# Six chunks of the first batch requested at once, mixing weights ahead of the stores, 17 unread products, and a second batch whose first stage is taken in another order

## The chip, the cores and the metric

The kernel runs on one core of a Trainium2 chip. A core has TensorE (matrix products, PE), VectorE (DVE), ScalarE (ACT), GpSimd (POOL) and SyncE (SP), which here issues nearly all transfers; 16 DMA engines carry them out. Each engine works through its own instructions in order, and semaphores tell one engine of another's progress. The metric is the device time of one execution in microseconds; less is better.

## The reference

`x` has 8 batches of 2496 rows by 256 columns. Each batch goes through a Fourier transform along its rows, a complex mix of the columns with a bias, a soft threshold and the inverse transform. The rows that come out go each to the best of eight experts.

```python
X = np.fft.rfft(x, axis=1)
Yr = Xr @ w_r - Xi @ w_i + b_r
Yi = Xr @ w_i + Xi @ w_r + b_i
Yr = np.sign(Yr) * np.maximum(np.abs(Yr) - 0.01, 0.0)   # Yi likewise
y = np.fft.irfft(Yr + 1j * Yi, n=2496, axis=1)
...
logits = x @ w_gate + modality_bias[modality_id]        # x: all rows of y
e_idx = np.argmax(logits, axis=1)
out[mask] = gate_w[mask, None] * (np.maximum(x[mask] @ w1[e], 0.0) @ w2[e])   # for each expert e
```

All values are float32.

## The kernel before, in words

The first part of the program does the transforms, the mix and the routing for batch after batch; the second part runs 78 tiles of expert products. The change lies in the start of the first part, which handles batches 0 and 1.

The 2496 points are split as 39 x 64. **Stage 1** (`s1_chunk`, products on L254) transforms over the 39. It uses that rows n and 39 - n go in as a sum and a difference: the host lays the rows out in pairs (`fold_rows`), `fold_load` brings a chunk of them (L221), and `fold` makes sum (VectorE, L233) and difference (L234, on VectorE for odd chunks and on GpSimd for even ones). A batch has six chunks: chunk 0 has one row pair a partition, the others two. The sum of a chunk is written into a part of the tile of the chunk before it that is no longer needed. Chunk tiles come from the pool `wx` with five buffers, so a sixth request waits until one is free. ScalarE copies the products of a chunk to `ev` (L256), and after each odd chunk SyncE stores them to the scratch tensor `scr` in DRAM (L262): four stores after chunk 1, four after chunk 3, six after chunk 5.

**Stage 2** works on ten pairs of frequencies a batch. `a_load` brings the rows of a pair back from `scr` (L275), with four buffers; the rows of any pair need all stores of the batch. `s2_pair` multiplies them by a part of the table `c_m` (L284); ScalarE and VectorE take the result apart into `Us`, `Xh` and `Xl` (L291 to L294). `mix_shared` (L307) and `mix_own` (L315) are the complex mix with the weights `wmix_r` and `wmix`, `shrink` is the threshold (L322, L323), and `is2_group` (L338, product `zs`) starts the inverse with a part of the table `c_q`. What follows in each batch (L352 to L409) ends the inverse and prepares the routing.

The mixing weights are made by `consts_mix`, a generator: its first part asks for `w_r`, `w_i` and the two biases, each bias being one row that is read once for each of 128 partitions; its second part is seven VectorE instructions (L203 to L208).

What sets the order: on TensorE, ScalarE, VectorE and GpSimd the order is that of the code in `build` (a manual schedule). On SyncE a scheduler places the transfers, bound by the data and by `issue_after`, which puts a request behind a named one. Five chunks of batch 0 are asked for first; chunk 5 and the first part of `c_m` behind the first four stores; chunks 0 to 3 of batch 1 between and behind further stores; then weights, biases and the first rows of stage 2. The code that follows takes chunks 0 to 2 of batch 1 between the first pairs, and the loop `for g in range(5)` takes chunks 3, 4 and 5 in its passes 0, 1 and 2, one a pass, behind `s2` of pairs 4, 6 and 8.

Of the kernel before, what the change touches and what calls it, by code (L numbers as in the profile page):

```python
# [23 lines left out]
D = 256  # L24
# [104 lines left out]
def fold_rows(x):  # L129
# [3 lines left out]
    out = np.zeros((nb, 128, 2, J1, d), x.dtype)  # L133
    for h in range(2):
        for g in range(3):
            p, o = HF * h + 21 * g, (3 * h + g) * J1
            n = min(J1, N2 - o)
            out[:, p:p + K1, 0, :n] = x[:, :K1, o:o + n]
            out[:, p + 1:p + 1 + K1, 1, :n] = x[:, :N1 - 1 - K1:-1, o:o + n]
    return out  # L140


class Attn:
# [5 lines left out]
    def pools(self, ctx):  # L149
# [5 lines left out]
        self.wx = pool("wx", 5)  # L155
# [38 lines left out]
    def consts_mix(self):  # L194
# [5 lines left out]
        for i, nm in enumerate(("b_r", "b_i")):  # L200
            nc.sync.dma_start(self.bias[:, i, :], I[nm].rearrange("(o d) -> o d", o=1).to_broadcast([128, 256]))
        yield
# [14 lines left out]
    def fold_load(self, b, c):  # L217

        lo, hi = max(0, 2 * c - 1), 2 * c + 1
        self.xt[b, c] = self.wx.tile([128, 2, 2, D], F32, tag="x", name=f"x_{b}_{c}"), hi - lo  # L220
        return self.nc.sync.dma_start(self.xt[b, c][0][:, :, :hi - lo, :], self.I["x"][b, :, :, lo:hi, :])  # L221

    def fold(self, b, c):
# [5 lines left out]
        a, z = (x[:, i, :n].rearrange("p j d -> p (j d)") for i in range(2))  # L229
# [968 lines left out]
def build(tc, I, out, nb):  # L1198
    nc = tc.nc
    with ExitStack() as outer:  # L1200
        dp = outer.enter_context(tc.tile_pool(name="wsp", bufs=1, space=DRAM))
        wsp = dp.tile([E * 128, 8192], F32, name="wsp")
        with ExitStack() as ctx:
# [7 lines left out]
            def spare(name):  # L1211
                pool = next(rooms)
                if pool is at.wx:
                    return pool.tile([128, 2, 2, D], F32, tag="x", name=name).rearrange("p i j d -> p i (j d)")
# [33 lines left out]
            for c in range(5):  # L1248
                first = at.fold_load(0, c)
            at.fold(0, 0)  # L1250
            at.fold(0, 1)
            mixing = at.consts_mix()
            for c in range(6):
                at.s1_chunk(0, c)
                at.fold(0, c + 2)
                with tc.issue_after(at.stored.ins if c else first.ins):
                    if c == 1:
                        at.fold_load(0, 5)
                        at.table_load("m", 0)
                    elif c == 3:  # L1260
                        at.fold_load(1, 0)
                        at.fold_load(1, 1)
                    elif c == 5:
                        at.fold_load(1, 2)
                        ins = at.fold_load(1, 3)
            with tc.issue_after(at.stored.ins):
                next(mixing, None)
                for i in range(3):
# [245 lines left out]
```

## Time and profile before

| | us |
|---|---|
| median of 3 runs | 1478.58 |
| lowest and highest | 1478.58, 1480.11 |
| profiled execution | 1481.04 |
| its span, first to last instruction | 1479.3 |
| TensorE busy in it | 1399.1 (95%) |
| VectorE, ScalarE, GpSimd busy | 774.5, 580.1, 552.6 |

The span is cut into stretches by the starts of named steps. What counts in a stretch is how long TensorE waited in it, for whom, and which of its two clock levels was granted: a clock of 1.00 means 2.4 GHz, of 0.50 means 1.2 GHz, and a value between them is a mean over the stretch. A DMA share of 1 means that all 16 engines had packets under way all the time. Times in the profile count from the first instruction.

### The profile page before, as it was taken

Reading aid. Unit: us, or ns where it says so; the run is one execution under the profiler, and the core shown is the slowest. Engines: PE = TensorE matmul, PEld = TensorE weight load, DVE = VectorE, ACT = ScalarE, POOL = GpSimd, SP = SyncE. Lnnn points to the kernel's source line nnn. Section 1 sums busy time; section 2 is a strip of 40 time slices with the busy share of each in tenths; the row PEclk is TensorE's granted clock in tenths of the full one; section 3 lists DMA queues with packets and bytes.
Section 4 is the critical chain, followed back from the end, with each engine's and each line's share of the span. In section 5 each row is a group of like instructions: output and inputs, shape, how many; then the busy total and the mean of one; then the engine's idle time right before and its main releaser. Section 6 shows DMA issues by size and latency. Waiting matters only on the chain. (4 is left out here: it accounts for less than half of the span.)

```text
span 1479.3 us, 34745 instructions
## 1 busy us (share of the span) xinstructions
PE 1399.1 (95%) x13058; PEld 1264.6 (85%) x13058; DVE 774.5 (52%) x1427; ACT 580.1 (39%) x1127; POOL 552.6 (37%) x562
## 2 busy tenths in 40 slices
PE   3899999999999896999999999999999999999998
PEld 1777685859586783999998999999999999999998
DVE  2567766656666774555664554554343433434332
ACT  2445454554545462333343333333232333323332
POOL 1012555556465554555232332232222323223222
PEclk7899999999999997999999999999999999999999
DMA  8745464545545475765565688883522222264520
GB/s 254 229 128 179 137 193 135 180 148 162 168 147 155 153 274 158 260 190 162 165 197 144 172 255 252 269 252 67 161 45 44 59 44 48 54 207 119 159 45 31
DMA packets 305163, 229.34 MB, mean 155 GB/s; under 512 B 203998, under 2 KB 259040, under 8 KB 302432
## 3 DMA queue, kind: packets, MB, share of 16 engines
q1 hardware_dynamic: 285120, 185.46, 44.4%
q0 software_dynamic: 19872, 41.61, 7.9%
q8 instruction: 105, 1.72, 0.5%
q14 instruction: 66, 0.54, 0.1%
HBM read 417.59 MB, written 112.54 MB: 358 GB/s over the span
## 5 line engine op out<-in xcount | busy, mean ns | idle before, releaser
L948 PE MATMUL y<-w,hh 128*128 128x256 f32 x2496 | 431.8, 277 | 1.9 <-DMA w<-wsp 1.6
L918 PE MATMUL h<-xh,w 128*128 128x256 f32 x2496 | 402.4, 278 | 6.5 <-DMA w<-wsp 3.6
L948 PEld LDWEIGHTS y<-w,hh 128*128 128x128 f32 x2496 | 376.7, 188 | 4.3 <-issue 2.1
L918 PEld LDWEIGHTS h<-xh,w 128*128 128x128 f32 x2496 | 339.1, 189 | 8.7 <-issue 4.2
L948 PE MATMUL y<-w,hl 128*128 128x256 f32 x1248 | 345.9, 277 | 0.4 <-issue 0.2
L573 POOL DMA_INDIRECT xs<-x,si x256 | 257.0, 1004 | 224.3 <-PE bk L398 45.4
L921 DVE SCALAR_TENSOR_TENSOR hl<-h,hh 128x512 fp32r<-128x512 f32 x312 | 214.6, 690 | 170.2 <-ACT hh L920 121.8
L920 ACT ACTIVATE hh<-h 128x512 fp32r<-128x512 f32 x312 | 185.9, 599 | 259.9 <-PE h L918 247.7
L963 POOL DMA_INDIRECT out<-o,ix x157 | 154.6, 984 | 326.7 <-ACT o L940 286.0
L918 PE MATMUL h<-xl,w 128*128 128x256 f32 x1248 | 245.2, 278 | 0.0
L948 PEld LDWEIGHTS y<-w,hl 128*128 128x128 f32 x1248 | 234.3, 188 | 0.9 <-DVE hl L921 0.4
L938 DVE TENSOR_SCALAR o<-y,xt 128x256 f32<-128x256 f32 x78 | 37.8, 484 | 299.3 <-ACT o L940 295.2
L918 PEld LDWEIGHTS h<-xl,w 128*128 128x128 f32 x1248 | 189.4, 189 | 0.2 <-DVE xl L899 0.2
L899 POOL TENSOR_TENSOR xl<-tr,xh 128x512 fp32r<-128x512 f32 x72 | 93.2, 1295 | 242.0 <-ACT xh L898 242.0
L940 ACT ACTIVATE o<-y,xt 128x256 f32<-128x256 f32 x78 | 37.1, 476 | 282.0 <-PE y L948 279.2
L315 PE MATMUL mx<-wmix,Xh 128*128 128x256 f32 x640 | 106.4, 289 | 1.9 <-issue 1.2
L284 PE MATMUL s<-c_m,a 128*128 128x128 f32 x640 | 87.6, 281 | 17.1 <-DMA a<-scr 14.1
L284 PEld LDWEIGHTS s<-c_m,a 128*128 128x128 f32 x640 | 82.0, 194 | 22.9 <-issue 18.1
L315 PEld LDWEIGHTS mx<-wmix,Xh 128*128 128x128 f32 x640 | 87.5, 192 | 14.7 <-issue 8.9
L338 PE MATMUL zs<-c_q,s 64*128 64x128 f32 x1280 | 85.2, 282 | 6.2 <-ACT z L342 4.8
L889 DVE STREAM_TRANSPOSE tr<-xt 128x512 f32<-128x512 f32 x78 | 90.1, 1155 | 0.0
L338 PEld LDWEIGHTS zs<-c_q,s 64*128 64x128 f32 x1280 | 76.6, 191 | 12.6 <-ACT z L342 4.9
(213 smaller groups left out, 1482.2 us busy)
## 6 DMA issues: line engine op xcount, KB each, us to landing
w<-wsp SPq DMA_DIRECT2D x152, 2048.0 KB
wsp<-wr SPq DMA_DIRECT2D x64, 512.0 KB
x<-in_x SPq DMA_DIRECT2D x40, 512.0 KB
a<-scr SPq DMA_DIRECT2D x80, 256.0 KB
xt<-xs SPq DMA_DIRECT2D x312, 64.0 KB
wr<-in_moe_w SPq DMA_DIRECT2D x64, 256.0 KB
scr<-ev SPq DMA_DIRECT2D x48, 240.0 KB
pw<-in_moe_w SPq DMA_DIRECT2D x8, 1024.0 KB
```

The costliest lines, as they stand in the source:

```text
L284: self.done = nc.tensor.matmul(ps[:, c, :, i, :], at[:, i, c * 128:(c + 1) * 128], self.m[:, k1 * 128:(k1 + 1) * 128].rearrange("p (r k) - ...
L315: self.done = self.nc.tensor.matmul(ps[:, i, :], t[:, c, 1 - i, :], self.w[:, i, c, lo, :], start=False, stop=n == len(ops) - 1, skip_grou ...
L338: self.done = nc.tensor.matmul(ps[i][:, h, c, :], s[rows, r, c * 128:(c + 1) * 128], self.q[rows, o:o + 128], start=r == 0, stop=r == 1)
L573: i = self.nc.gpsimd.indirect_dma_start(out=self.xs, out_offset=bass.IndirectOffsetOnAxis(ap=si[:, k:k + 1], axis=0), in_=rows, in_offset= ...
L889: nc.vector.transpose(tr.rearrange("p c (t s) -> p c s t", t=32), t.rearrange("p (s c e) -> p c s e", c=2, e=32))
L899: (nc.gpsimd if i > 5 else nc.vector).tensor_sub(xl, tr, xh)
L918: self.done = nc.tensor.matmul(ps[:, q, :], w1[:, lo, c, f * 128:(f + 1) * 128], x[:, c, :], start=n == 0, stop=n == 5)
L920: nc.scalar.activation(hh[:, 2 * p:2 * p + 2, :], ps, AF.Relu)
L921: nc.vector.scalar_tensor_tensor(hl[:, 2 * p:2 * p + 2, :], ps, 0.0, hh[:, 2 * p:2 * p + 2, :], ALU.max, ALU.subtract)
L938: nc.vector.tensor_scalar_mul(o[:, s, :], y[s], gate)
L948: nc.tensor.matmul(y[s], lhsT, w2[:, lo, f, :], start=n == 0, stop=n == 23)
L963: ins = self.nc.gpsimd.indirect_dma_start(out=self.out, out_offset=bass.IndirectOffsetOnAxis(ap=ix, axis=0), in_=o, in_offset=None, bounds ...
```

## The change

`fold_rows` lays out x so that a chunk is one run of 4 KB a partition (2 KB for chunk 0) instead of two runs, and the host does that ahead of the kernel. `wx` has six buffers. All six chunks of batch 0 are asked for at the start; behind them come the first part of `c_m`, the weights and the biases, and only then the stores. Behind chunk 5 TensorE does 17 products of `c_m` with itself (`warm`) into a PSUM tile that nobody reads. Of batch 1 nothing is asked for until the rows of pair 2 are; its chunks 0 and 1 come behind `s2` of pair 3, chunks 2 to 5 in the passes 0 and 1 of the loop, two a pass.

```diff
-        self.wx = pool("wx", 5)
+        self.wx = pool("wx", 6)
...
-        self.xt[b, c] = self.wx.tile([128, 2, 2, D], F32, tag="x", name=f"x_{b}_{c}"), hi - lo
-        return self.nc.sync.dma_start(self.xt[b, c][0][:, :, :hi - lo, :], self.I["x"][b, :, :, lo:hi, :])
+        self.xt[b, c] = self.wx.tile([128, 4 * D], F32, tag="x", name=f"x_{b}_{c}"), hi - lo
+        return self.nc.sync.dma_start(self.xt[b, c][0][:, :2 * (hi - lo) * D], self.I["x"][b, :, 2 * lo * D:2 * hi * D])
...
-        t, self.room = self.room[:, :n * D], x[:, 0].rearrange("p j d -> p (j d)")
+        t, self.room = self.room[:, :n * D], x[:, 2 * D:] if n == 1 else x[:, :2 * D]
...
+    def warm(self, n):
+
+        ps = self.ps.tile([128, 512], F32, tag="z", name="warm")
+        for _ in range(n):
+            self.nc.tensor.matmul(ps[:, :256], self.m[:, :128], self.m[:, :256], start=True, stop=True)
...
-            for c in range(5):
-                first = at.fold_load(0, c)
+            for c in range(6):
+                ins = at.fold_load(0, c)
+
+            def then(f, *args):
+                nonlocal ins
+                with tc.issue_after(ins.ins):
+                    ins = f(*args)
+
+            mixing = at.consts_mix()
+            then(at.table_load, "m", 0)
+            then(next, mixing)
             at.fold(0, 0)
             at.fold(0, 1)
-            mixing = at.consts_mix()
             for c in range(6):
                 at.s1_chunk(0, c)
                 at.fold(0, c + 2)
-                with tc.issue_after(at.stored.ins if c else first.ins):
...
+            ins = at.stored
+            at.warm(17)
+            next(mixing, None)
+            for f, *args in ((load, 0), (load, 1), (at.table_load, "q", 0), (load, 2), (at.table_load, "m", 1),
+                             (at.fold_load, 1, 0), (at.fold_load, 1, 1), (load, 3), (at.table_load, "m", 2),
+                             (at.fold_load, 1, 2), (at.fold_load, 1, 3), (at.fold_load, 1, 4), (at.fold_load, 1, 5)):
+                then(f, *args)
...
+            s2(0)
+            bias(0)
+            s2(1)
+            bias(1)
+            shared(0)
             s2(2)
+            shared(1)
             mix(0)
             bias(2)
+            at.fold(1, 0)
             mix(1)
             bias(3)
             s2(3)
+            at.fold(1, 1)
+            at.s1_chunk(1, 0)
+            at.fold(1, 2)
+            at.s1_chunk(1, 1)
+            at.fold(1, 3)
...
-                    if b == 0 and g < 3:
-                        at.s1_chunk(1, g + 3)
-                        at.fold(1, g + 5)
+                    if b == 0 and g < 2:
+                        at.s1_chunk(1, 2 * g + 2)
+                        at.fold(1, 2 * g + 4)
...
+                    if b == 0 and g < 2:
+                        at.s1_chunk(1, 2 * g + 3)
+                        at.fold(1, 2 * g + 5)
```

In the names below the first number behind `x`, `a`, `s1`, `s2` or `ev` is the batch, the second the chunk or pair, the last only numbers the tile. SyncE's requests from the last stores of batch 0 on, before:

```order
L262 DMA scr_0_147<-ev_0_4_1_208 60x2x256 x2
L262 DMA scr_0_147<-ev_0_4_0_207 60x4x256 x2
L262 DMA scr_0_147<-ev_0_4_1_208 40x2x256 x2
L221 DMA x_1_2_231<-in_x 128x2x512
L221 DMA x_1_3_233<-in_x 128x2x512
L198 DMA wmix_r_127<-in_w_r 128x2x256
L199 DMA st_w0_235<-in_w_i 128x2x256
L201 DMA bias_129<-in_b_r 128x256
L201 DMA bias_129<-in_b_i 128x256
L275 DMA a_0_0_241<-scr_0_147 128x2x256
```

And now, from the weights on:

```order
L200 DMA wmix_r_127<-in_w_r 128x2x256
L201 DMA st_w0_145<-in_w_i 128x2x256
L203 DMA bias_129<-in_b_r 128x256
L203 DMA bias_129<-in_b_i 128x256
L264 DMA scr_0_156<-ev_0_0_0_157 60x3x256 x2
L264 DMA scr_0_156<-ev_0_0_1_158 60x3x256 x2
L264 DMA scr_0_156<-ev_0_2_0_183 60x4x256 x2
L264 DMA scr_0_156<-ev_0_2_1_184 60x4x256 x2
L264 DMA scr_0_156<-ev_0_4_1_210 60x2x256 x2
L264 DMA scr_0_156<-ev_0_4_0_209 60x4x256 x2
L264 DMA scr_0_156<-ev_0_4_1_210 40x2x256 x2
L283 DMA a_0_0_258<-scr_0_156 128x2x256
```

Weights and biases have moved from behind the stores to ahead of them, and between the last store and the rows of pair 0 (`a_0_0`) there is no request any more. TensorE behind the last products of stage 1 of batch 0, before:

```order
L254 MATMUL s1_0_5_1_218<-x_0_5_174,c_s_123 64x512
L254 MATMUL s1_1_0_0_263<-xs_1_255,c_s_123 64x256
L254 MATMUL s1_1_0_1_264<-xs_1_255,c_s_123 64x256
L254 MATMUL s1_1_0_0_263<-x_1_0_203,c_s_123 64x256
L254 MATMUL s1_1_0_1_264<-x_1_0_203,c_s_123 64x256
L284 MATMUL s2_0_0_273<-c_m_121,a_0_0_241 128x2x64 x4
L254 MATMUL s1_1_1_0_294<-x_1_0_203,c_s_123 64x512
L254 MATMUL s1_1_1_1_295<-x_1_0_203,c_s_123 64x512
L254 MATMUL s1_1_1_0_294<-x_1_1_205,c_s_123 64x512
L254 MATMUL s1_1_1_1_295<-x_1_1_205,c_s_123 64x512
L307 MATMUL mx_0_0_292<-wmix_r_127,Us_0_0_278 128x256 x2
L284 MATMUL s2_0_1_313<-c_m_121,a_0_1_244 128x2x64 x4
```

And now:

```order
L256 MATMUL s1_0_5_1_220<-x_0_5_142,c_s_123 64x512
L277 MATMUL warm_233<-c_m_121 128x256 x17
L292 MATMUL s2_0_0_285<-c_m_121,a_0_0_258 128x2x64 x4
L292 MATMUL s2_0_1_299<-c_m_121,a_0_1_260 128x2x64 x4
L315 MATMUL mx_0_0_297<-wmix_r_127,Us_0_0_290 128x256 x2
L292 MATMUL s2_0_2_316<-c_m_121,a_0_2_263 128x2x64 x4
L315 MATMUL mx_0_1_311<-wmix_r_127,Us_0_1_304 128x256 x2
```

Chunk 0 of batch 1 is gone from the place ahead of pair 0, the unread products stand in it, and chunk 1 no longer parts pair 0 from pair 1. VectorE around the first two thresholds of batch 0, now (before, the folds of chunks 0 to 2 of batch 1 stood ahead of pair 0, and that of chunk 3 behind the seven instructions of the weights):

```order
L331 SCALAR_TENSOR_TENSOR s_0_0_344<-mx_0_0_297,u_0_0_343 128x512
L235 TENSOR_TENSOR xs_1_349<-x_1_0_266 128x256
L331 SCALAR_TENSOR_TENSOR s_0_1_365<-mx_0_1_311,u_0_1_364 128x512
L301 TENSOR_TENSOR Us_0_3_375<-Us_0_3_375,s2_0_3_370 128x256
L302 TENSOR_TENSOR Xl_0_3_377<-s2_0_3_370,Xh_0_3_376 128x512
L235 TENSOR_TENSOR x_1_0_266<-x_1_1_268 128x512
L236 TENSOR_TENSOR x_1_1_268<-x_1_1_268 128x512
```

The fold of chunk 1 of batch 1 (the last two rows) has moved behind both thresholds and the steps of pair 3.

## Rows read from the trace of the kernel before

**Rows 1.** The page: busy time (share, instructions), and the costliest groups.

```profile
PE 1399.1 (95%) x13058; PEld 1264.6 (85%) x13058; DVE 774.5 (52%) x1427; ACT 580.1 (39%) x1127; POOL 552.6 (37%) x562
...
L284 PE MATMUL s<-c_m,a 128*128 128x128 f32 x640 | 87.6, 281 | 17.1 <-DMA a<-scr 14.1
```

**Rows 2.** TensorE's waits in 0 to 150: us in total, times, longest.

```profile
PE s L284 <- DMA a<-scr: 14.1, 2, 12.2
```

**Rows 3.** Stretches: length, busy time (instructions) of each engine, TensorE's clock, DMA share, GB/s.

```profile
2.50:10.40 7.90, 4.80 (x18) 1.49 (x20) 2.50 (x4) 0.80 (x3) 1.21 (x2) 1.00 0.88 295
10.40:12.40 2.00, 2.00 (x10) 0.42 (x8) 1.15 (x2) 0.98 (x3) 0.78 (x1) 1.00 0.33 86
12.40:26.00 13.60, 7.82 (x32) 1.84 (x28) 4.12 (x7) 4.88 (x10) 2.08 (x3) 0.70 0.94 291
...
28.00:31.50 3.50, 0.00 (x0) 0.00 (x0) 0.69 (x1) 0.00 (x0) 0.66 (x1) 0.50 1.03 373
31.50:36.00 4.50, 0.00 (x0) 0.00 (x0) 0.00 (x0) 0.00 (x0) 0.60 (x1) 0.50 1.02 200
...
37.19:59.97 22.78, 18.28 (x105) 13.72 (x105) 12.52 (x25) 8.95 (x20) 1.36 (x2) 0.83 0.70 220
60.00:87.08 27.08, 27.08 (x252) 23.52 (x248) 15.82 (x29) 15.09 (x31) 0.73 (x1) 1.00 0.66 190
87.08:92.85 5.77, 3.90 (x21) 3.90 (x21) 1.46 (x3) 0.86 (x2) 0.00 (x0) 0.70 0.91 291
```

**Rows 4.** Timeline, 12 to 42: start, length, instructions [idle before, who ended it].

```profile
12.67 0.69 DVE L233 TENSOR_TENSOR x<-x 128x512 f32<-128x512 f32 x1
...
18.52 0.69 DVE L233 TENSOR_TENSOR x<-x 128x512 f32<-128x512 f32 x1 [5.17 <-DMA x<-in_x]
...
19.36 2.68 PE L254 MATMUL s<-x,c_s 64*64 64x512 f32 x8 [3.53 <-DVE x L233]
19.60 5.70 SPq L262 DMA_DIRECT2D scr<-ev  x6
...
28.97 0.38 SPq L275 DMA_DIRECT2D a<-scr  x1
...
37.19 2.04 PE L284 MATMUL s<-c_m,a 128*128 128x128 f32 x8 [12.23 <-DMA a<-scr]
...
41.08 1.40 PE L307 MATMUL mx<-wmix_r,Us 128*128 128x256 f32 x4
```

**Rows 5.** Timeline of TensorE, 62 to 73: one group of work without a wait.

```profile
62.82 1.05 PE L284 MATMUL s<-c_m,a 128*128 128x128 f32 x8
63.80 2.06 PE L338 MATMUL zs<-c_q,s 64*128 64x128 f32 x32
65.78 1.99 PE L307 MATMUL mx<-wmix_r,Us 128*128 128x256 f32 x8
67.61 1.05 PE L284 MATMUL s<-c_m,a 128*128 128x128 f32 x8
68.60 1.09 PE L254 MATMUL s<-x,c_s 64*64 64x512 f32 x8
69.62 0.74 PE L315 MATMUL mx<-wmix,Xh 128*128 128x256 f32 x4
...
72.47 1.05 PE L284 MATMUL s<-c_m,a 128*128 128x128 f32 x8
```

**Rows 6.** Timeline, 79 to 95, SyncE and TensorE; and SyncE's longest wait there.

```profile
80.03 3.30 SPq L262 DMA_DIRECT2D scr<-ev  x4
...
86.14 0.90 SPq L275 DMA_DIRECT2D a<-scr  x2
...
88.95 1.66 PE L284 MATMUL s<-c_m,a 128*128 128x128 f32 x8 [1.87 <-DMA a<-scr]
...
94.30 0.94 PE L284 MATMUL s<-c_m,a 128*128 128x128 f32 x7
...
SPq L221 <- PE s L254: 7.8, 2, 7.2
```

More of the change, by code (lines that the diff above doesn't have):

```diff
@@ L132, in fold_rows @@
     x = x.reshape(nb, N1, N2, d)
-    out = np.zeros((nb, 128, 2, J1, d), x.dtype)
+    out = np.zeros((nb, 128, J1, 2, d), x.dtype)
     for h in range(2):
@@ L137, in fold_rows @@
             n = min(J1, N2 - o)
-            out[:, p:p + K1, 0, :n] = x[:, :K1, o:o + n]
-            out[:, p + 1:p + 1 + K1, 1, :n] = x[:, :N1 - 1 - K1:-1, o:o + n]
-    return out
+            out[:, p:p + K1, :n, 0] = x[:, :K1, o:o + n]
+            out[:, p + 1:p + 1 + K1, :n, 1] = x[:, :N1 - 1 - K1:-1, o:o + n]
+    for j in range(1, J1, 2):
+        out[:, :, j:j + 2] = out[:, :, j:j + 2].transpose(0, 1, 3, 2, 4).copy()
+    return out.reshape(nb, 128, J1 * 2 * d)
 class Attn:
@@ L200, in consts_mix @@
         for i, nm in enumerate(("b_r", "b_i")):
-            nc.sync.dma_start(self.bias[:, i, :], I[nm].rearrange("(o d) -> o d", o=1).to_broadcast([128, 256]))
-        yield
+            ins = nc.sync.dma_start(self.bias[:, i, :], I[nm].rearrange("(o d) -> o d", o=1).to_broadcast([128, 256]))
+        yield ins
         V.scalar_tensor_tensor(ws, self.wr, -1.0, wi, ALU.mult, ALU.subtract)
@@ L228, in fold @@
         x, n = self.xt.pop((b, c))
-        a, z = (x[:, i, :n].rearrange("p j d -> p (j d)") for i in range(2))
+        a, z = (x[:, i * n * D:(i + 1) * n * D] for i in range(2))
         if c == 0:
             self.room = self.w6.tile([128, 512], F32, tag="xs", name=f"xs_{b}")
-        t, self.room = self.room[:, :n * D], x[:, 0].rearrange("p j d -> p (j d)")
+        t, self.room = self.room[:, :n * D], x[:, 2 * D:] if n == 1 else x[:, :2 * D]
         nc.vector.tensor_add(t, a, z)
@@ L1255, in build @@
                 at.fold(0, c + 2)
-                with tc.issue_after(at.stored.ins if c else first.ins):
[L1257 to L1268, printed above, removed]
-                    ins = load(i)
-                    if i < 2:
-                        with tc.issue_after(ins.ins):
-                            ins = at.fold_load(1, 4) if i else at.table_load("q", 0)
+            ins = at.stored
[5 more added lines that the diff above has]
+                then(f, *args)
             with tc.issue_after(ins.ins):
-                at.table_load("m", 1)
                 rt.load_ids(0)
-            at.fold(1, 0)
-            at.fold(1, 1)
-            for c in range(3):
-                with tc.issue_after(ins.ins):
-                    at.s1_chunk(1, c)
-                at.fold(1, c + 2)
-                if c == 1:
-                    with tc.issue_after(ins.ins):
-                        at.fold_load(1, 5)
-                if c == 0:
-                    s2(0)
-                    next(mixing, None)
-                    bias(0)
-                if c == 1:
-                    shared(0)
-                    s2(1)
-                    bias(1)
-                if c == 2:
-                    shared(1)
-            ins = load(3)
-            with tc.issue_after(ins.ins):
-                at.table_load("m", 2)
+            s2(0)
[3 more added lines that the diff above has]
+            shared(0)
             s2(2)
+            shared(1)
             mix(0)
             bias(2)
+            at.fold(1, 0)
             mix(1)
```

2 lines of the change are left out of this document (1 added, 1 removed).

## The prediction

> **What bounds the kernel now.** I read the page first. TensorE is busy 1399.1 us of the 1479.3 us span [rows 1], so a start that costs less TensorE idle time shifts everything behind it, unless something later waits for more than TensorE. The page's group for the second stage (L284) shows the only large DMA wait of the attention part: 14.1 us for `a<-scr` in the whole run [rows 1]; the waits of the first 150 us hold the same 14.1 us, in two waits, the longest 12.2 us [rows 2]. So both stand in the start, and no later batch waits for its rows. The timeline shows them: TensorE reaches 37.19 after 12.23 us of waiting for `a_0` of batch 0 [rows 4], and 88.95 after 1.87 us for `a_0` of batch 1 [rows 6]. From 62.82 to 72.47 it runs without a gap [rows 5], and the whole stretch 60.00 to 87.08 is like it (27.08 of 27.08 us busy at clock 1.00) [rows 3].
>
> Why the first wait is long: the DMA engines have only share 0.33 in 10.40 to 12.40, since chunk 5 isn't asked for yet, and are then full [rows 3]. Chunk 5 is folded only at 18.52, and the last store is asked for by 25.30; `a_0`, asked for at 28.97, comes 8.2 us later, behind four chunks of batch 1, the mixing weights and the biases [rows 4]. In 31.50 to 36.00, where weights and biases pass, the engines are full at only 200 GB/s [rows 3]. On an emptier queue `a_0` of batch 1 needs 2.8 us, 86.14 to 88.95 [rows 6]. The granted clock is at its lower level (0.50) after the first hole, and its mean over 37.19 to 59.97 is 0.83 [rows 3].
>
> **The change, part by part.** The profiled run took 1481.04 us against a median of 1478.58; I work out a difference in its trace and take it from the median. Behind `s2` of pair 0 of batch 1 the instructions of TensorE, VectorE and ScalarE stand in the same order as before (numbers apart), so the yardstick is when TensorE starts that step: 88.95 now.
>
> *Six chunks at once.* The fold of chunk 4 stands at 12.67 without a wait, the one of chunk 5 at 18.52 after 5.17 us [rows 4]. Asked for at once, chunk 5 follows chunk 4 by 1.8 us (512 KB at the 295 GB/s of 2.50 to 10.40) [rows 3]; it should be folded by 14 to 15. From that fold to the last product took 3.5 us (18.52 to 22.04), 2.68 of them at half clock [rows 4]; so stage 1 of batch 0 ends at about 17 instead of 22.
>
> *When the first `a` comes.* Ahead of it now stand (KB by the shapes in the order) 2816 of x, 64 + 256 of tables, 512 of weights, 256 of biases, 2560 of stores: 6464 KB, 6.62 MB. Before, 1792 KB of batch 1 stood there too; these are gone from the path. At 291 GB/s, which 12.40 to 26.00 shows for mixed loads and stores [rows 3], they take 22.7 us; from 2.5, where the first loads run full, that is 25.2. The slow 4.5 us at 200 GB/s cost 4.5 x (1 - 200/291) = 1.4 us more, and the weights and biases still come, only sooner: 26.6. Then `a_0` must wait for the last store to land. In batch 1 its request stood 2.8 us behind the end of the last store's issue (83.33 to 86.14) [rows 6], with that store's own transfer in it; I take half, 1.4 us: 28.0. Then 2.8 us to TensorE [rows 6]: 30.8, against 37.19. Bounds: all at 373 GB/s (28.00 to 31.50) [rows 3] gives 2.5 + 17.7 + 1.4 + 2.8 = 24.4; all at 200 GB/s gives 39.8. I take 30.8, because 12.40 to 26.00 is the row with the same stores in it. The Trainium skill's "DMA: Bandwidth & Descriptors", section "Where 436 GB/s comes from", lets the HBM side bind at about 358 GB/s per core. The row with 373 GB/s is a little above that, so here the measurement decides, and by the page's figure, as an estimate, `a_0` would come at 25.2.
>
> *Unread products.* 17 products of 128x256. Four such products take 1.83 us (65.78 to 67.61) [rows 5], so 17 take 7.8 us, 17 to 24.8, in a hole that lasts to 30.8: no cost; cover is 6.0 us. If `a_0` came at 24.4 they would cost 0.4 us; at half clock, 15.6 us, they would end at 32.6 and cost 1.8. What they buy is clock, and only if the hole behind them is short: in the trace a wait of 3.53 us was followed by products at half speed (19.36, 2.68 us for eight, against 1.09 at 68.60) [rows 4, 5], and 1.87 us by some too (88.95) [rows 6]. With 6.0 us left, I expect the lower clock at `a_0` all the same.
>
> *Mixing weights.* Seven VectorE instructions, each at most 0.69 us (the 512-wide add at 12.67) [rows 4], so under 4.8 us, move from behind `s2` of pair 0 into the hole; they need the biases, which land by about 19. Hidden there.
>
> *TensorE from `a_0` on.* Prices by the starts in [rows 5]: `s2` 0.98, `zs` group 1.98, a pair of shared products 1.83, a chunk of stage 1 1.02, two mixes 2.85; a group of all of them (two `s2`) is 9.65, 62.82 to 72.47. Between the two yardsticks stand 5 groups less two `zs` groups and one pair of mixes, plus half a chunk (chunk 0 of batch 1, which was done in the hole before): 48.25 - 3.96 - 2.85 + 0.5 = 41.9 us.
>
> What is lost beside that: 37.19 to 59.97 took 22.8 us for 14.5 us of such work (five `s2`, three chunks, four shared, two mixes), so 8.3 us went to waits and clock. Now: two `s2` at half clock, 2.04 against 1.05 [rows 4, 5]: 2.0 us. The wait for ScalarE and VectorE ahead of the first shared product (39.23 to 41.08) [rows 4] is covered by `s2` of pair 1 but for some 0.3. New is a wait in chunk 1 of batch 1: its fold stands on VectorE behind both shrinks and pair 3's two steps, seven instructions or about 4.3 us after mix 0 and its 0.7 us ScalarE step, while TensorE has only a mix, an `s2` and half a chunk, 2.9 us: 2.1 us of wait. Behind it on TensorE stand the shared products of pairs 2 and 3. Sum 4.4; bounds 2.0 (clock alone) and 8.3 (as before).
>
> Is `a_4` there in time? Between `a_0` and it stand 4608 KB (rows `a`, tables, all of batch 1's x), 16.2 us at 291 GB/s: from 28.0 to about 45.5 with its landing. TensorE wants it at 30.8 + 11.9 + 4.4 = 47.1. Just in time; at 200 GB/s it would be 6 us late.
>
> *Chunk 5 of batch 1 before `s2` of pair 7.* That is one group, 9.65 us, sooner, while the second wait is 1.87 us; and SyncE no longer sits 7.2 us with a chunk's request (waiting for a buffer) ahead of stores [rows 6]. The wait goes, and so do the half-clock products behind it: 88.95 to 94.30 took 5.35 us against 0.98 + 2.85 = 3.83, so 1.5 us more. What is late next is nothing that the trace shows.
>
> Sum: TensorE is at the yardstick at 30.8 + 41.9 + 4.4 = 77.1, 11.85 us sooner, plus 1.5: 13.4 us. 1478.58 - 13.4 = **1465.2 us** (1467.6 in an execution like the profiled one). 4 KB rows of x in later batches hide behind TensorE and count nothing. Later short stretches at the lower clock may fall otherwise once all is shifted: some 3 us either way.
>
> **Rivals.**
> (B) *The queue runs at its best.* At 373 GB/s `a_0` is there at 24.4, the unread products end at 24.8, there is no hole and no half clock (2.4 lost): 24.8 + 41.9 + 2.4 = 69.1, 19.9 + 1.5 = 21.4 us gained: 1457.2. For it: [rows 3] show that rate for pure loads. Against: never with stores.
> (C) *The weights hold up the stores, then batch 1's x holds up the rows.* With the queue slow, 34 to 36 for `a_0` and up to 6 us for `a_4`: at 35, T = 35 + 41.9 + 4.4 = 81.3, gain 9.2, less 3 for `a_4`: 1472.4. For it: biases pass at 200 GB/s. With 200 GB/s throughout and 8.3 lost, T = 39.8 + 50.2 = 90.0, and 1.5 comes back: 1478.1, so the change would not do what it says.
> (E) *Slower.* In every later batch x requests stand ahead of the stores on SyncE. If one of them waits for its buffer as the one of 7.2 us did [rows 6], `a_0` of the next batch is late and TensorE pays what it paid at 88.95, 1.87 + 1.5 = 3.4 us, in each of six batches: 20.4 - 13.4 = 7 us slower, 1485.6. It decides from four such batches on. Against: no later batch waits for `a` now [rows 1, 2], and with six buffers a chunk takes over the same chunk's buffer of the batch before, which is read sooner.
>
> **How the numbers follow.** The forecast (1461.5 to 1469) gets 0.62, B (down to 1457) 0.13, C 0.14, no effect 0.04, E 0.07. 1457 to 1473 holds the first two and most of C. Times within 0.2%, about 3 us, are what a measurement can't tell from no change: faster 0.88, same 0.05, slower 0.07.
>
> **What would show it.** Chunk 5 folded by 15; 17 products from about 17 to 25; the first second-stage product near 31 with clock 0.5 around it; a 2 us wait in chunk 1 of batch 1 for VectorE; no wait for `a` in batch 1; that step at about 77. I am wrong if the first `a` comes after 35, if `s2` of pair 4 waits for DMA, or if later batches begin to wait for `a<-scr`.

## The result and the profile after

The changed kernel takes 1460.38 us (median of 6 runs, 1459.10 to 1465.56), the kernel before 1477.40 us beside it on the same chip (6 runs, 1473.05 to 1480.11). The ratio is 0.9896, 95% interval 0.9879 to 0.9913: 12.9 to 17.9 us faster, where 13.4 were forecast. The profiled execution took 1459.84 us with a span of 1458.0.

TensorE's timeline (start, length, instructions, idle before and who ended it), to be held against [rows 4] and [rows 6]:

```profile
15.92 7.61 PE L277 MATMUL warm<-c_m 128*128 128x256 f32 x34
28.00 3.49 PE L292 MATMUL s<-c_m,a 128*128 128x128 f32 x16 [4.47 <-DMA a<-scr]
...
32.43 1.05 PE L292 MATMUL s<-c_m,a 128*128 128x128 f32 x8
...
37.35 1.05 PE L292 MATMUL s<-c_m,a 128*128 128x128 f32 x8
...
42.01 2.60 PE L256 MATMUL s<-x,c_s 64*64 64x512 f32 x8 [2.85 <-DVE x L235]
44.55 2.40 PE L315 MATMUL mx<-wmix_r,Us 128*128 128x256 f32 x8
46.78 1.05 PE L292 MATMUL s<-c_m,a 128*128 128x128 f32 x8
...
76.91 1.05 PE L292 MATMUL s<-c_m,a 128*128 128x128 f32 x8
...
80.63 1.06 PE L292 MATMUL s<-c_m,a 128*128 128x128 f32 x8
```

The first rows of stage 2 are taken up at 28.00 instead of 37.19. The yardstick, `s2` of pair 0 of batch 1, stands at 76.91 instead of 88.95, without a wait in front of it. The next pair stands at 80.63 instead of 94.30: 13.67 us sooner.

TensorE's longest waits in 0 to 150, and the page's group for stage 2, against [rows 2] and [rows 1]:

```profile
PE s L256 <- DVE xs L235: 4.7, 1, 4.7
PE s L292 <- DMA a<-scr: 4.5, 1, 4.5
PE s L256 <- DVE x L235: 2.8, 1, 2.8
```

```profile
L292 PE MATMUL s<-c_m,a 128*128 128x128 f32 x640 | 87.1, 280 | 8.7 <-DMA a<-scr 4.5
```

The wait for `a` has gone from 14.1 us in two pieces to 4.5 us in one. A new one of 2.8 us stands in front of chunk 1 of batch 1 (the row at 42.01). The 4.7 us are the first load of the run, which was there before.

The same stretch on ScalarE and SyncE shows a wait that the prediction did not have:

```profile
9.25 14.07 SPq L264 DMA_DIRECT2D scr<-ev  x14
...
12.50 1.07 ACT L258 COPY ev<-s 128x512 f32<-128x512 f32 x2 [0.38 <-PE s L256]
...
18.25 0.58 ACT L258 COPY ev<-s 128x512 f32<-128x512 f32 x1 [4.68 <-DMA scr<-ev]
19.28 1.56 ACT L258 COPY ev<-s 128x512 f32<-128x512 f32 x3 [0.44 <-DMA scr<-ev]
25.11 0.91 SPq L283 DMA_DIRECT2D a<-scr  x2
```

TensorE is through with stage 1 of batch 0 at 16.0, but ScalarE copies the products of chunks 4 and 5 only from 18.25 to 20.84. It waits for a buffer: `ev` has four, each filled by two chunks, so chunk 4 needs one back from the first stores. These were asked for from 9.25 on, but stood in the queue behind the weights and biases.

Stretches (length, busy time of TensorE, its weight loads, VectorE, ScalarE and GpSimd, TensorE's clock, DMA share, GB/s), against [rows 3]:

```profile
2.50:11.60 9.10, 6.66 (x30) 2.00 (x32) 4.11 (x7) 2.27 (x6) 1.98 (x2) 1.00 1.00 366
11.60:17.10 5.50, 5.33 (x27) 1.89 (x22) 3.14 (x5) 1.59 (x4) 1.35 (x2) 1.00 0.98 233
17.10:25.10 8.00, 6.43 (x30) 5.32 (x28) 2.48 (x5) 2.15 (x4) 0.00 (x0) 1.00 0.76 240
25.10:28.00 2.90, 0.00 (x1) 0.00 (x1) 0.00 (x0) 0.00 (x0) 0.00 (x0) 1.00 0.56 174
```

The chunks of x come at 366 GB/s, weights and biases at 233. From 17.1 on the DMA engines have gaps (0.76), since the last stores are still to be copied (e9 below takes that wait away, and the gaps with it).

### The profile page after: what moved, and what is told of

It reads as the page before. It is cut to its first block, busy times and chain, and to the rows that moved or that the text cites. A ratio compares the mean times of both kernels' runs of the same rounds, so it can differ in the third digit from the quotient of the medians.

```text
span 1458.0 us, 34783 instructions
## 1 busy us (share of the span) xinstructions
PE 1400.0 (96%) x13092; PEld 1266.3 (87%) x13092; DVE 775.0 (53%) x1427; ACT 579.5 (40%) x1127; POOL 551.4 (38%) x562
```

## The experiments

All edits are to the changed kernel unless another is named. They ran on four other chips of the same kind; the kernel before takes 1433 to 1437 us there, some 40 us less. So each ratio is to the kernel before on the same chip. The times of the start, which differ by 1 us or less between the two chips that ran the changed kernel, are compared directly; of the kernel before there is only the trace of the first chip. "Rows" is the start of the first `s2`, "pair 3" and "pair 4" that of the fourth and fifth, all from TensorE's timeline.

| kernel | rows | pair 3 | pair 4 | yardstick | ratio to before |
|---|---|---|---|---|---|
| before | 37.2 | 53.3 | 58.0 | 89.0 | 1 |
| after, first chip | 28.0 | 37.3 | 46.8 | 76.9 | 0.9896 [0.9879, 0.9913] |
| c1_after, the same again | 27.0 | 37.4 | 47.2 | 77.5 | 0.9895 [0.9877, 0.9914] |
| e7_six_alone | 34.2 | 48.8 | 53.4 | 82.8 | 0.9982 [0.9973, 0.9992] |
| e8_batch1_first | 32.0 | 41.4 | 50.8 | 80.9 | 0.9953 [0.9938, 0.9968] |
| e3_weights_behind | 29.2 | 39.3 | 49.0 | 79.1 | 0.9913 [0.9887, 0.9939] |
| e2_two_runs | 28.2 | 37.6 | 47.1 | 77.3 | 0.9893 [0.9856, 0.9929] |
| e1_no_warm | 26.8 | 37.1 | 46.9 | 77.2 | 0.9926 [0.9902, 0.9949] |
| e6_warm27 | 28.9 | 38.1 | 47.9 | 78.0 | 0.9931 [0.9911, 0.9950] |
| e4_chunk5_late | 27.1 | 36.4 | 47.1 | 77.8 | 0.9894 [0.9861, 0.9927] |
| e5_folds_early | 26.9 | 37.0 | 46.3 | 76.5 | 0.9912 [0.9895, 0.9929] |
| e9_six_ev | 26.1 | 34.6 | 42.8 | 73.0 | 0.9892 [0.9872, 0.9912] |
| f1_shared_first | 26.8 | 35.9 | 42.2 | 73.1 | 0.9888 [0.9869, 0.9908] |
| f2_both | 26.3 | 35.4 | 41.7 | 72.6 | 0.9875 [0.9852, 0.9897] |

The intervals of the ratios are 3 to 10 us wide. Single edits are therefore told apart by the yardstick; the ratio only says whether a run as a whole agrees.

### The control

> The changed kernel again, unchanged, on the chip of the other three, so that they have a trace beside them from the same chip. Theory (the start is set by the program, the rest of the run by the chip): the first second-stage product at 27 to 28.3, the yardstick (the second stage of pair 0 of batch 1) at 76.5 to 78, as on the first chip, and 0.987 to 0.991 of the kernel before. Rival (the chip changes the start too): the yardstick moves by more than 1.5 us.

The yardstick came at 77.5 and the rows at 27.0. Five runs have the same code up to the rows (after, c1, e4, e5 and f1), and their rows lie between 26.8 and 28.0. Between the two runs of the whole code the yardstick differs by 0.5 us, but the way from the rows to it by 1.5 (48.9 and 50.4): the two differences cancel. What is smaller than this is called scatter below.

### What brought the first rows forward

Three edits share the gain: six chunks at once, the weights ahead of the stores, and the x of batch 1 behind the rows. e7 does the first alone, in the kernel before:

```diff
-        self.wx = pool("wx", 5)
+        self.wx = pool("wx", 6)
...
-            for c in range(5):
+            for c in range(6):
...
-                        at.fold_load(0, 5)
```

> The kernel before with one part of the change alone: six buffers, and chunk 5 of batch 0 asked for with the other five. My theory says that the gain comes from what stands in the queue ahead of the first rows, and that chunk 5 alone is worth its idle DMA time (about 1.5 us) and the end of stage 1: the first rows come 1 to 4 us sooner than 37.2, and the time falls by 1 to 5 us against before. Rival (the six chunks are the change; the rest is decoration): 10 us or more are gained.

The rows come 2.9 us sooner (34.2) than in the trace of before, the yardstick 6.2. The run as a whole gains only 1.8 us (1431.52 against 1433.34). Where the other 4 us went isn't shown: the kernel before has no trace on that chip. By either number most of the gain of the whole change is not in this edit.

e8 puts the x of batch 1 back to where it was, and leaves the rest of the change:

```diff
-            for f, *args in ((load, 0), (load, 1), (at.table_load, "q", 0), (load, 2), (at.table_load, "m", 1),
-                             (at.fold_load, 1, 0), (at.fold_load, 1, 1), (load, 3), (at.table_load, "m", 2),
-                             (at.fold_load, 1, 2), (at.fold_load, 1, 3), (at.fold_load, 1, 4), (at.fold_load, 1, 5)):
+            for f, *args in ((at.fold_load, 1, 0), (at.fold_load, 1, 1), (at.fold_load, 1, 2), (at.fold_load, 1, 3),
+                             (load, 0), (load, 1), (at.table_load, "q", 0), (load, 2), (at.table_load, "m", 1),
+                             (load, 3), (at.table_load, "m", 2), (at.fold_load, 1, 4), (at.fold_load, 1, 5)):
```

> The changed kernel with chunks 0 to 3 of batch 1 (1792 KB) asked for ahead of the first rows of stage 2, as the kernel before had them, instead of behind them. Theory (the prediction's largest term: these bytes are paid in the time of the first rows): 1.84 MB at 291 to 366 GB/s are 6.3 to 5.0 us, so the first second-stage product comes at 32 to 34 instead of 27 to 28; the lower clock is granted there, and the yardstick comes 4 to 7 us later than 77, at 81 to 84. Rival (the queue has room: a DMA share of 0.76 in 17.1 to 25.1 and 0.56 in 25.1 to 28.0 leaves 3.2 us of it unused): the rows come at 30 or sooner, 3 us or less later, and since the x of batch 1 is then there, the yardstick loses 2 us or less.

Stretches of this run, columns as above:

```profile
17.10:25.10 8.00, 6.92 (x33) 5.74 (x31) 2.48 (x5) 2.15 (x4) 0.00 (x0) 1.00 0.79 237
25.10:28.00 2.90, 0.00 (x0) 0.00 (x0) 0.00 (x0) 0.00 (x0) 0.00 (x0) 1.00 1.01 349
28.00:36.00 8.00, 4.05 (x18) 4.01 (x19) 1.02 (x2) 1.37 (x4) 0.00 (x0) 0.57 1.05 384
```

The rows come at 31.95, 4.9 us later than the control's 27.03 and 3.9 later than on the first chip, and the DMA engines are full from 25.1 on. These 1792 KB (1.84 MB) so cost 4 to 5 us, where the theory had 5.0 to 6.3: its mechanism, at a somewhat lower price. The empty time in the queue that the rival counts on is there and is used (a share of 1.01 in 25.1 to 28.0, where the changed kernel had 0.56), but it is far from enough. The yardstick loses 3.5 us, since chunk 1 of batch 1 waits no less but the time behind the rows is 1.4 us shorter. So of the 10.2 us between 37.2 and 27.0, six chunks alone are 2.9, the x of batch 1 is 4 to 5, and 2 to 3 are left for the rest together; that the parts simply add up wasn't tried.

e3 moves weights and biases back behind the stores:

```diff
             then(at.table_load, "m", 0)
-            then(next, mixing)
...
             at.warm(17)
+            then(next, mixing)
             next(mixing, None)
```

> The changed kernel with the mixing weights and biases asked for behind the last store of batch 0 instead of ahead of the first one; the rest of the order is the same. My working says that they stand in the stores' way for 3.5 to 4.5 us, while behind the last store the queue runs empty until the rows are asked for. If so, the last store lands 3 to 4 us sooner, and the first rows, behind the weights in the queue, come at 24 to 26 instead of 28.0; gain 2 to 3.5 us, unless the weights then come too late for the mixes (they must be made by about 33). Rival (asking for them ahead is what made the change fast, because behind the stores they hold up the rows as they did before): the rows come at 28 or later, same or slower.

ScalarE and SyncE of this run:

```profile
14.54 1.07 ACT L258 COPY ev<-s 128x512 f32<-128x512 f32 x2 [1.04 <-PE s L256]
...
15.95 1.07 ACT L258 COPY ev<-s 128x512 f32<-128x512 f32 x2 [0.33 <-PE s L256]
19.89 0.42 SPq L200 DMA_DIRECT2D wmix_r<-in_w_r  x1
...
22.34 0.89 SPq L283 DMA_DIRECT2D a<-scr  x2
```

The wait of ScalarE is gone: the last copy starts at 15.95, the rows are asked for at 22.34 instead of 24.28 in the control. But their way takes 6.8 us, behind weights and biases, where it took 2.75. The rows end up 1.2 to 2.1 us later than in the two runs of the changed kernel, and the yardstick 1.7 to 2.2. The theory (rows at 24 to 26) missed, and the rival held: weights ahead of the stores hold the stores up, and it is still the better place.

e2 has the old layout of x, two runs a partition for a chunk:

```diff
-    out = np.zeros((nb, 128, J1, 2, d), x.dtype)
+    out = np.zeros((nb, 128, 2, J1, d), x.dtype)
...
-        return self.nc.sync.dma_start(self.xt[b, c][0][:, :2 * (hi - lo) * D], self.I["x"][b, :, 2 * lo * D:2 * hi * D])
+        t = self.xt[b, c][0][:, :2 * (hi - lo) * D].rearrange("p (i j d) -> p i j d", i=2, d=D)
+        return self.nc.sync.dma_start(t, self.I["x"][b, :, :, lo:hi, :])
```

> The changed kernel with the old layout of x in DRAM, so that a chunk is again two runs of 2 KB a partition instead of one of 4 KB; the order on all engines is the same. I predicted the first rows at 30.8 and they came at 28.0; chunk 5 landed about 2 us sooner than the rate of the kernel before allowed. If the longer runs are the cause, chunk 5 is folded 1.5 us or more later than in the changed kernel and the first rows come at 29.5 to 31. Rival (the layout does nothing; the rest of the queue was only faster than I reckoned): the first rows come at 28.0 within 0.5 us, and the time is the changed kernel's.

The rows at 28.2 are 0.2 us behind the latest of the five above, the yardstick at 77.3 lies between the two runs of the same code. The layout is worth nothing that can be seen here.

### What holds the last stores

e9 takes the wait of ScalarE away by giving `ev` room:

```diff
-        self.w3 = pool("w3", 4)
+        self.w3 = pool("w3", 6)
```

> The changed kernel with six instead of four buffers for the evacuated products of stage 1 (ev). In the changed kernel ScalarE copies the products of chunks 4 and 5 of batch 0 only at 18.25 to 20.84, after 4.68 us of waiting for the landing of the first stores, which pass behind the weights and biases. Theory (this wait sets the last store, and so the first rows): the copies come right behind the products, before 17, the last store is asked for 3 us sooner, the DMA engines no longer fall to a share of 0.76 behind 17.1, and the first rows come 1.0 to 1.9 us sooner (0.24 of the 8.0 us is all that can be won); the yardstick follows by as much, the ratio falls by about 0.001. Rival (the bytes ahead of the rows set them, the copies wait in their shade): the first rows move by less than 0.5 us.

ScalarE and the rows of this run, then stretches of the control and of this run:

```profile
13.90 1.07 ACT L258 COPY ev<-s 128x512 f32<-128x512 f32 x2 [0.85 <-PE s L256]
...
15.35 1.08 ACT L258 COPY ev<-s 128x512 f32<-128x512 f32 x2 [0.38 <-PE s L256]
23.17 0.90 SPq L283 DMA_DIRECT2D a<-scr  x2
...
26.08 2.05 PE L292 MATMUL s<-c_m,a 128*128 128x128 f32 x16 [3.22 <-DMA a<-scr]
```

```profile
16.00:21.50 5.50, 5.50 (x27) 4.86 (x26) 2.48 (x5) 2.15 (x4) 0.00 (x0) 1.00 0.89 296
...
27.00:36.00 9.00, 8.90 (x45) 8.23 (x45) 3.74 (x8) 3.24 (x9) 0.00 (x0) 0.69 1.03 363
36.00:48.00 12.00, 9.22 (x52) 6.15 (x52) 6.97 (x12) 4.40 (x10) 1.99 (x2) 0.86 0.96 327
```

```profile
16.00:21.50 5.50, 5.50 (x27) 4.85 (x26) 2.39 (x5) 0.43 (x1) 0.00 (x0) 1.00 1.02 357
21.50:24.00 2.50, 1.36 (x7) 0.85 (x5) 0.00 (x0) 0.00 (x0) 0.00 (x0) 1.00 0.24 85
...
27.00:36.00 9.00, 8.37 (x65) 7.41 (x65) 5.16 (x11) 4.77 (x11) 0.73 (x1) 1.00 1.02 375
36.00:48.00 12.00, 9.22 (x68) 6.28 (x68) 7.68 (x14) 5.42 (x12) 2.66 (x3) 1.00 1.03 355
```

The copies end at 16.4, and the gaps are gone: from 16.0 to 21.5 the DMA engines are full (1.02) and move 357 GB/s, where the control has 0.89 and 296. All of that is stores: the last load asked for ahead of them, a bias, had landed at 15.9. Behind that they stand nearly idle up to 24.0 (0.24): the rows are asked for at 23.17, when the last store has landed. So the wait of ScalarE did space the stores. What it was worth is less sure: the rows are there 0.95 us sooner than the control's, just under the theory's range. The two runs with six buffers (26.1 here, 26.3 in f2) are 0.5 to 1.9 us ahead of all five with the changed kernel's code up to there.

The yardstick is 4.4 us sooner than the control's. Only 0.95 of that lies ahead of the rows; behind them the clock stayed at 1.00 from 27 to 48, where the control was granted 0.69 and 0.86. Those 3.5 us are the price of the lower clock in this start. Whether the edit kept the clock up isn't shown: TensorE waited 3.22 us for its rows here and 4.01 in the control, but f1, without the edit, kept it too.

### What the unread products bought

e1 takes them out, e6 makes them 27:

```diff
-            at.warm(17)
```

> The changed kernel without its 17 unread products, all else as changed. There TensorE did them from 15.9 to 23.5 and then waited 4.5 us for the first rows of stage 2, which came at 28.0, and the granted clock fell just then, at 28.3. My theory (the gain is the earlier rows; the products buy a little clock only): the rows still come at 28.0, the first two second-stage products take about 4.0 us instead of 3.5 and the lower clock lasts one or two steps longer, so the step s2 of pair 0 of batch 1 starts 1 to 2.5 us later (78 to 79.4 instead of 76.9) and the time is about 1462. Rival (the products carry the gain): without them the start runs at half clock as it did before the change, 5 us or more are lost, 1465.5 or above.

```diff
-            at.warm(17)
+            at.warm(27)
```

> The changed kernel with 27 unread products instead of 17, which fill the hole up to about 28.0. My theory (the hole of 4.5 us behind the products is what lets the clock fall): the clock stays up at the first rows, the first two second-stage products take 2.0 us instead of 3.5, and 1.5 to 2.5 us are gained, part of which the fold of chunk 1 takes back. Rival (the clock falls anyway, or the products run over and delay the first rows): same within 1 us, or up to 1 us slower.

From the rows to the yardstick it is 50.4 us without them, 50.4 in the control, 48.9 on the first chip and 49.0 in e2: against these they bought between nothing and 1.5 us. Without them the lower clock was granted from 18.7 to 32.4, with them in the control from 25.8 to 32.7: TensorE has nothing to do in the part that they save, and in both the first rows meet the lower clock. That is not so in every run with 17 products: in f1, whose code up to the rows is the control's, and in e9 and f2 the clock stayed at 1.00. Whether the products made that possible is open, since none of these was run without them.

With 27 the clock is at 1.00 for the first rows and falls behind the wait in front of chunk 1 (0.86 in 36 to 48); from the rows to the yardstick it is 49.1 us. But the rows themselves came at 28.9, and the yardstick stands at 78.0. The products did not delay the rows, for TensorE had waited 1.2 us by then. SyncE asked for the last store by 24.35 and for the rows at 26.12, where the control has 22.49 and 24.28; why is not shown. The ratios of both, 0.9926 and 0.9931, are 4 to 5 us worse than the control's, of which the start explains at most 0.5; the intervals overlap, and nothing follows from that.

### What the second batch's chunks bring

e4 takes chunk 5 of batch 1 back to its old place, one pass later:

```diff
+                    if b == 0 and g == 2:
+                        at.s1_chunk(1, 5)
...
-                    if b == 0 and g < 2:
+                    if b == 0 and g < 1:
                         at.s1_chunk(1, 2 * g + 3)
```

> The changed kernel with chunk 5 of batch 1 at its old place behind s2 of pair 8, one group of work later; SyncE's order stays. My theory puts 3.4 us of the gain on that move (1.87 us of waiting for the first rows of batch 1 and 1.5 us of half clock behind it). In the changed kernel those rows were asked for at 71.7 and there at 74.6, and wanted at 76.9. One group later the stores are 6 to 8 us later, so TensorE waits 3 to 6 us for them and the clock falls behind that: 4 to 7 us slower, about 1465 to 1467. Rival (the wait went because everything else in the start is sooner, not because of this move): no wait of TensorE for a at that place, same time.

A wait for `a` of 0.23 us comes back at the yardstick, which stands at 77.8 against 77.5, and the next pair at 81.6 against 81.2. The prediction gave this move 1.87 + 1.5 = 3.4 us. From pair 4 on it is 30.6 us to the yardstick against 30.2 in the control, so the move is worth some 0.4. What took the wait of before away is to be seen in e7, which has chunk 5 of batch 1 at its old place too. Its only wait for `a` up to 150 us is that for the first rows:

```profile
PE s L284 <- DMA a<-scr: 10.5, 1, 10.5
```

There the sixth buffer and the early request alone are new, and SyncE waits at most 0.3 us with a request of x between 60 and 95, where it waited 7.2 before [rows 6].

e5 puts the folds of chunks 0 and 1 of batch 1 ahead of the first mix, so that VectorE has them out of the way:

```diff
             shared(1)
+            at.fold(1, 0)
+            at.fold(1, 1)
             mix(0)
             bias(2)
-            at.fold(1, 0)
...
             s2(3)
-            at.fold(1, 1)
             at.s1_chunk(1, 0)
```

> The changed kernel with the folds of chunks 0 and 1 of batch 1 ahead of mix 0 on VectorE instead of behind the two thresholds. I forecast a wait of 2.1 us of TensorE for VectorE in chunk 1 of batch 1; the changed kernel shows 2.85 us there (42.01), and the lower clock from 42.0 to 45.4 behind it. If the place of the fold is the cause, the wait goes below 0.5 us and s2 of pair 4 starts 3 to 4.5 us sooner (42.3 to 43.8 instead of 46.8); of that as much is kept as its rows are there in time (they landed at 42.3): about 1457. Rival (the rows of chunk 1 or of pair 4 are what is late): TensorE waits as long, only for DMA.

One of TensorE's waits of this run, then ScalarE's copies of chunk 0's products and the fold of chunk 1 (on VectorE) in the changed kernel, then the copies in this run:

```profile
PE s L256 <- ACT ev L258: 2.8, 1, 2.8
```

```profile
40.10 0.66 ACT L258 COPY ev<-s 128x256 f32<-128x256 f32 x2
...
41.18 0.68 DVE L235 TENSOR_TENSOR x<-x 128x512 f32<-128x512 f32 x1
```

```profile
40.96 0.66 ACT L258 COPY ev<-s 128x256 f32<-128x256 f32 x2
```

The fold now ends at 37.5, and chunk 1 still waits 2.76 us: for ScalarE, which has yet to copy the products of chunk 0 out of the two PSUM banks that chunk 1 needs. But the edit itself made ScalarE late. The folds stand ahead of the first threshold on VectorE, ScalarE's next steps wait for that threshold, and its copies come 4.0 us behind the start of pair 3 (40.96 against 36.99) instead of 2.75 (40.10 against 37.35). In the changed kernel these copies are done at 40.8, while the fold that chunk 1 waits for ends at 41.9. So the fold is what ends the wait there. With it out of the way and ScalarE where it was, some 1.3 of the 2.85 us would stay (TensorE is free at 39.2, the first of the two copies ends at about 40.4): an estimate from these rows, and no run has it.

f1 leaves both as they are and asks instead what TensorE could do meanwhile. The shared products of pairs 2 and 3 go ahead of chunk 1 (and are left out where the loop had them):

```diff
             at.s1_chunk(1, 0)
+            shared(2)
+            shared(3)
             at.fold(1, 2)
             at.s1_chunk(1, 1)
```

> The changed kernel with the shared products of pairs 2 and 3 ahead of chunk 1 of batch 1 instead of behind it. Theory (the 2.8 us in front of chunk 1 are a wait in which other work of TensorE is ready: Us of pair 2 is made by 34.8, its bias is copied at 37.6; Us of pair 3 is made by 40.7): about 1.8 us of the wait are filled, the products behind it keep the higher clock (1.7 us of half-clock loss go), pair 4 starts 3 to 3.7 us sooner, at about 43.3, if its rows (42.3) are there, and the yardstick comes 2.5 to 3.7 us sooner; ratio 0.002 lower than the control's. Rival (the rows of pairs 4 to 7 or ScalarE's order are late next, as when the folds were put ahead): a new wait for DMA or ScalarE between 42 and 60 and a yardstick less than 1 us sooner.

f2 has this and the six buffers.

> Both edits together: six ev buffers, and the shared products of pairs 2 and 3 ahead of chunk 1 of batch 1. Theory (they are separate waits, 25 to 28 and 39 to 46): the yardstick is sooner by the sum of what each gives, 3.5 to 5.5 us, ratio 0.0025 to 0.004 lower than the control's. Rival (rows of pair 4, which come in the queue behind batch 1's x, are the next limit): the first rows come sooner, but pair 4 waits for DMA and the yardstick is sooner by no more than with the shared products alone.

TensorE in the control, and in f2:

```profile
37.42 1.05 PE L292 MATMUL s<-c_m,a 128*128 128x128 f32 x8
...
42.09 2.47 PE L256 MATMUL s<-x,c_s 64*64 64x512 f32 x8 [2.78 <-DVE x L235]
44.49 2.88 PE L315 MATMUL mx<-wmix_r,Us 128*128 128x256 f32 x8
47.21 1.05 PE L292 MATMUL s<-c_m,a 128*128 128x128 f32 x8
```

```profile
35.40 1.05 PE L292 MATMUL s<-c_m,a 128*128 128x128 f32 x8
...
37.22 1.13 PE L315 MATMUL mx<-wmix_r,Us 128*128 128x256 f32 x4
38.77 1.13 PE L315 MATMUL mx<-wmix_r,Us 128*128 128x256 f32 x4 [0.43 <-DVE Us L301]
40.06 1.71 PE L256 MATMUL s<-x,c_s 64*64 64x512 f32 x8 [0.16 <-DVE x L235]
41.70 1.16 PE L292 MATMUL s<-c_m,a 128*128 128x128 f32 x8
```

The wait of 2.8 us becomes two of 0.4 and 0.2, and the products behind it run at the higher clock. In f1 it is 37.2 us from pair 3 to the yardstick against 40.0 in the control: 2.8 us, within the theory's 2.5 to 3.7. This stretch scatters little: the eight runs with the order of the changed kernel in it and the lower clock behind chunk 1 have 39.5 to 40.0. Not all of it need be the edit's. In e9, which lacks the edit, the clock stayed up there as well, and it is 38.4 us: at equal clock the order of the products gives 1.2, and the other 1.6 are the clock. Whether the shorter waits kept it up isn't shown; e6, which had the higher clock at the first rows and waits 2.8 us in front of chunk 1, lost it there. The other 1.5 of f1's 4.4 us lie ahead of pair 3 and are nearly all the clock again, which its edit does not touch.

f2 is at the yardstick 0.5 us ahead of f1, which is scatter, and 4.9 ahead of the control. That lies in its theory's range, but not by its sum: alone the edits gave 4.4 us each, most of it the same clock, which counts once. Its pair 4 does not wait for rows. With 1416.72 us against the control's 1420.11, and 0.9875 [0.9852, 0.9897] of the kernel before, it is the best version run, though its interval overlaps the control's; that it beats the changed kernel rests on the yardstick. The drops of the ratio that were expected of e9, f1 and f2 (0.001 to 0.004) are smaller than the intervals can show.

## Why the prediction was right, and where two of its steps were wrong

The forecast of the yardstick, 77.1, met 76.9 and 77.5. It did so with two errors that cancel (2.8 us too late at the first rows, 2.6 too little lost behind them), and that is luck. The measured time, 1460.38 us, lies 1.1 us below the band of the forecast (1461.5 to 1469), in that of rival B, though B's queue at its best did not come about.

*First rows, forecast 30.8, measured 28.0.* The term of the queue, 6.62 MB at 291 GB/s from 2.5, gave 25.2, and `a_0` was asked for at 25.11. The mean rate came out right, but none of its parts: 366, 233 and 240 GB/s in the three stretches make 6.5 MB. The two additions of 1.4 us did occur: against 291 GB/s the stretch with weights and biases lost some 1.1 us (5.5 us at 233), and the one with the gaps in the stores and the landing of the last some 1.4 (8.0 us at 240). The step that failed is the price of x. What passed up to 11.6 (3.3 MB, about what x and the two tables have) ran at 366, and so took some 2.3 us less than at 291, a rate read from a row with stores in it. (These three are estimates from the stretches above.) The last term, 2.8 us from the request to TensorE, was 2.89. By the figure of the Trainium skill's "DMA: Bandwidth & Descriptors", section "Where 436 GB/s comes from", about 358 GB/s, the rows would have come at 25.2, as an estimate. The loads of x ran slightly above it (366), and the stores of e9, without gaps, at 357; but the mean up to the request was 289, so for the sum the row with the same stores in it was the better price.

*Loss beside work, forecast 4.4, measured 7.0* (76.91 - 28.00 - 41.9). Up to pair 3 it is 9.35 us for 7.62 of work, 1.7 lost, against 2.3 forecast. The 0.3 in that forecast rest on a wrong reading. The stretch 39.23 to 41.08 of the kernel before isn't a wait; the products of chunk 1 of batch 1 fill it:

```profile
39.17 1.99 PE L254 MATMUL s<-x,c_s 64*64 64x512 f32 x8
```

From pair 3 to pair 4 it is 9.43 us for 4.33 of work, 5.1 lost, against 2.1. Behind pair 4 it is 0.2. The wait in front of chunk 1 of batch 1 was forecast with its place and its cause (VectorE's fold behind both thresholds) and measured 2.85. The term that I missed is what follows it: 2.60 us for eight products that take 1.09 elsewhere, and 2.40 for the shared ones. In e9, at a clock of 1.00, the same two take 1.71 and 1.99, and pair 3 to pair 4 takes 8.14, so the half clock is 1.3 of the 5.1. I had put that price on the first rows and not on a wait that I had just found. The rest of chunk 1's excess, which e9 has too, is the fold's second step on VectorE, which ends 0.6 us behind the start of the chunk's first product.

*Chunk 5 of batch 1.* No wait for `a` is left in batch 1, as forecast. Of the two reasons given, the place of chunk 5 fell with e4: the move is worth some 0.4 us, not 3.4. The other held: SyncE no longer sits with a request of x in front of the stores, and with that alone the wait is gone in e7. So the 1.87 + 1.5 us do vanish, through the sixth buffer.

*Held as forecast:* chunk 5 folded by 14.9, stage 1 done at 16.0 (forecast 17), 17 products in 7.61 us without delay to anything, the lower clock at the first rows all the same, no wait for the rows of pair 4 at 46.78. The mixing weights' work on VectorE was hidden. That their transfers hold up the stores through ScalarE's four `ev` buffers was not foreseen beyond rival C, whose mechanism is there (e3 and e9) and is outweighed: x came faster than its price.

*Rivals.* B's rate did not come with the stores of the changed kernel in the queue (240 GB/s); in e9 they passed at 357, and even there the rows stood at 26.1 and not at 24.4. E's wait in later batches does not exist (the one wait for `a` of the page is that at 28.0). Against C, the rows were at 28.0 and not at 35.

*From the yardstick to the end.* The sum explains 13.7 us of the 17.0 between the medians, and of 21.3 between the profiled spans. Behind 100 us the granted clock was at its lower level for 41.6 us in the trace of before and for 26.8 us in that of after; if half of such time is lost, the difference is up to 7 us, which is about what is missing in the profiled pair. That these stretches fall as they do by the change, and not by chance, isn't shown: in the control, the same code, it is 19.2 us. The prediction allowed 3 us for them either way.

## What to carry to other kernels

A mean rate can come out right although none of its parts does. Here one price for all bytes hid that loads with no store beside them pass faster (366 GB/s) and that the stretch with the stores has gaps (240); price each part by the nearest row of its own kind, and slow pieces and landings may then be added. When loads go ahead of stores, look for who gets its buffers back from these stores: here ScalarE stood 4.7 us for them, and two more buffers ended it. And where an engine waits, ask first what it has further down that is ready: moving one engine's work away from the wait (e5) made the next engine late in its turn, moving ready work into it (f1) gave 2.8 us, 1.2 of them at equal clock.

## What the runs showed of the hardware that was not expected

The length of a hole does not say by itself whether the clock falls. In e9 TensorE waited 3.22 us for its rows and the clock stayed at 1.00; in e4 it waited 2.83 us and fell to the lower level. The wait of 2.8 us in front of chunk 1 was followed by the lower clock in the control and not in e9, which had not had it at the first rows either; but e6, which had not had it there either, lost it behind the same wait. What decides it stays open.

Stores passed as fast as loads where nothing spaced them: 357 GB/s in e9 from 16.0 to 21.5, at a DMA share of 1.02, against 366 for x in 2.5 to 11.6.

Chips of the same kind differ by 40 us on the same program. On the first chip TensorE had, at the same clock of 0.99, fewer instructions done in the same stretch than in the control, here after and then the control:

```profile
100.00:500.00 400.00, 379.86 (x4083) 289.51 (x4067) 267.64 (x544) 206.85 (x437) 214.93 (x233) 0.99 0.52 159
```

```profile
100.00:500.00 400.00, 393.56 (x4290) 306.39 (x4292) 287.43 (x585) 224.36 (x473) 227.45 (x245) 0.99 0.56 174
```

Its waits in the part before the expert products name "issue", that is, nothing that the profile shows, again after and then the control:

```profile
L346 PE MATMUL zs<-c_q,s 64*128 64x128 f32 x1280 | 84.9, 282 | 4.8 <-issue 4.8
```

```profile
L346 PE MATMUL zs<-c_q,s 64*128 64x128 f32 x1280 | 82.3, 278 | 0.7 <-ACT z L350 0.7
```

A single instruction takes nearly the same time (282 and 278 ns); the holes between them differ. The cause isn't known, and the ratio to the kernel before, 0.9896 and 0.9895, is not touched by it.
